# A decode layer on one core: the folded sum added in PSUM by an identity product, and the last columns split 192/64

## The chip, the core and the metric

The kernel runs on one core of a Trainium2 chip. The metric is the device time of one execution, in microseconds (us); of several runs the median is given. One core has five engines with instruction queues of their own: TensorE (PE in the profile; PEld is its weight load), VectorE (DVE), ScalarE (ACT), GpSimd (POOL) and SyncE (SP). They meet through semaphores. Data move between HBM and the on-chip memory SBUF by transfers (DMA) that SP and ACT issue here; products of TensorE are summed in PSUM, which has eight banks of 512 fp32 columns in 128 partitions.

## What is computed

One decode step of a transformer layer, all in fp32, for 8 sequences of one token and a model width of 1024:

```python
h  = x + attention(layernorm(x))      # 32 query heads, 4 key/value heads, window of 1024 keys
h2 = h + ffn(layernorm(h))            # h2 is the output, 8 x 1024

def ffn(x):                           # Dm = 1024, Df = 3584
    g = x @ w_gate
    u = x @ w_up
    return (gelu(g) * u) @ w_down     # the change lies at the end of this product
```

## The kernel before, in words

**Weights stream in, once.** The weights and the cache are laid out on the host in one array, in the order in which they are used. SP loads them through two halves of one SBUF tile `w` (`load`, L237): 14 large passes (`PASSES`, L28) that alternate between the halves, and behind them, without a wait, four small pieces for the rest of `w_down` (L259 to L261). A pass's load waits until the products of the pass two earlier are done (L239). The order on SP's queue is written out by hand, and so is that of every other engine.

**Products.** All matrix products have the small operand (8 rows, padded to 32) as weights and the streamed matrix as the moving operand. Four products sit side by side in the array, each with 32 output columns of its own, so that one "group" of four writes the four 32-partition quarters of a bank (`products`, L158). Such a product is called tiled here. fp32 takes two passes, and the trace shows each as a MATMUL of its own with a LDWEIGHTS before it. TensorE runs a loop of seven turns (L171 to L197), each with one pass of either half and eight transposes between them (L183). The transposes use the array whole (128 weights columns), so they are not tiled; only two of the seven turns use their results, which go to banks 4 and 5.

**The down product.** The 3584 rows of `w_down` are 28 chunks of 128 rows. Chunks 0 to 23 (`PAIRED = 24`) are the passes d0 and d1, in pairs of half the columns, so that their results must be folded: the upper 64 partitions of a bank hold, for the other half of the columns, what has to be added to the lower 64, and the other way round. The last four chunks, 24 to 27, come in the four small pieces, as "single row chunks": each of the four quarters of a bank gets 256 (`QW`) of the 1024 output columns, so nothing is folded. `PARTS = (2, 1)` says that the first piece has chunks 24 and 25, the second chunk 26. Chunk 27 is split by columns over the last two pieces: columns 0 to 159 of every quarter (`CUT = 160`) and columns 160 to 255. The semaphores of the four pieces are `s_dn[0]` to `s_dn[3]`.

**The end, before the change.**

- TensorE sums chunks 24 to 26 in bank 7 (L218 to L224, products at L221), then multiplies chunk 27 into bank 4 (160 columns) and bank 5 (96 columns), each after its own piece (L226 to L234, products at L229).
- `folded` (L384) puts the results of d0, d1 and the residual h together: two adds on DVE, a copy each on ACT (L389) and POOL (L390) that move halves across partitions, and an add on DVE into `pre` (L392, called at L459).
- DVE then adds bank 7 onto `pre` (L460), and adds `pre` and bank 4 into the first part of `o_fin` (L464), `pre` and bank 5 into the second (L466).
- ACT issues the output transfer of the first part (L480), SP that of the second (L483). ACT and POOL report to SP, which clears the semaphores and waits for both transfers (L485 to L488).

DVE's instructions are recorded and put down at the end, so all of them have the line L98 in the profile; they are told apart by tile and shape.

```python
226      for i, (b, c0, n) in enumerate(fin):      # fin = [(4, 0, CUT), (5, CUT, QW - CUT)]
...
230                  bank(b)[32 * j:32 * j + 32, 0:n], at_[:, rows - 1, :], w[:, at:at + n],
231                  start=True, stop=True), (s_dn[len(PARTS) + i], 16), inc=False)
```

Of the kernel before, what the change touches and what calls it, by code (L numbers as in the profile page):

```python
# [8 lines left out]
P = 128  # L9
# [7 lines left out]
NQ = 4  # L17
QW = D // NQ
# [1 line left out]
HB = B // 2  # L20
HALF = 16384
GAP = 144
CUT = 160

# [6 lines left out]
PAIRED = 24  # L33
PARTS = (2, 1)
# [81 lines left out]
def decode_block(nc, out, x, srcs, W):  # L116
# [3 lines left out]
    def sb(name, shape):  # L120
        return nc.alloc_sbuf_tensor(name, list(shape), F32).ap()

    first = nc.alloc_semaphore("first")
    pe = Engine(nc, nc.tensor, "pe")
    vector = Noted(nc.vector)
    dve = Engine(nc, vector, "dve")
    act = Engine(nc, nc.scalar, "act")
# [3 lines left out]

    s_in = [nc.alloc_semaphore(f"s_in{s}") for s in range(2)]
    s_dn = [nc.alloc_semaphore(f"s_dn{i}") for i in range(len(PARTS) + 2)]
    s_fin = nc.alloc_semaphore("s_fin")
    s_end = nc.alloc_semaphore("s_end")
    s_out = nc.alloc_semaphore("s_out")

    w = sb("w", [P, 2 * HALF])
    st = [sb(f"st{s}", [P, D + 32]) for s in range(2)]
    p_sb = sb("p", [P, W])  # L140
    ident = sb("ident", [P, P])
    at_ = sb("at", [P, DF // P, 32])
# [4 lines left out]
    def bank(i, n=1):  # L147
        return banks[:, i * N:(i + n) * N]
# [9 lines left out]
    def products(s, c):  # L158
        for j in range(NQ):
            at = block(s, c, j)  # L160
            ins = nc.tensor.matmul(  # L161
                bank(2 * s + c // 4)[32 * j:32 * j + 32, :],
                st[s][:, (c * NQ + j) * 32:(c * NQ + j + 1) * 32], w[:, at:at + N],
                start=(c % 4 == 0), stop=(c % 4 == 3))
        return ins
# [5 lines left out]
    with nc.body("turns", valid_engines=on_pe):  # L171
        closing = nc.tensor.mark_branch_hint_location()
        take(s_in[0], 17)
        for c in range(NC):
            if c == 4:
                take(s_half0, 16)
            ins = products(0, c)
        ins.then_inc(pe.sem, 1)
        take(s_p, 1)
        for h in range(2):  # L180
            for i in range(KC // 2):
                c = h * KC // 2 + i
                ins = nc.tensor.transpose(pp[h][:, i], p_sb[:, c * P:(c + 1) * P], ident)  # L183
            ins.then_inc(pe.sem, 1)
        take(s_in[1], 18)
        for c in range(4):
            if c == 3:
                take(s_half1, 16)
            ins = products(1, c)
# [3 lines left out]
    with nc.body("upper", valid_engines=on_pe):  # L193
        for c in range(4, NC):
            ins = products(1, c)
# [4 lines left out]
    def done(name):  # L200
        t, s = divmod(PASSES.index(name), 2)
        return (pe.sem, 5 * t + ((5 if t < TURNS - 1 else 4) if s else 1))
# [6 lines left out]
    rows = DF // P  # L209
    at = HALF + HALF // 2  # L210
    tail_at, place, of = [], [], []
    for i, n in enumerate(PARTS):
        tail_at.append(at)
        for k in range(n):
            place.append(at + k * D)
            of.append((s_dn[i], 16))
        at += n * D
    for q in range(PAIRED, rows - 1):  # L218
        for j in range(NQ):
            k = place[q - PAIRED] + j * QW  # L220
            ins = pe(lambda e: e.matmul(  # L221
                bank(7)[32 * j:32 * j + 32, 0:QW], at_[:, q, :], w[:, k:k + QW],
                start=(q == PAIRED), stop=(q == rows - 2)), of[q - PAIRED], inc=False)
    t_quads = pe.mark(ins)  # L224
    fin = [(4, 0, CUT), (5, CUT, QW - CUT)]
    for i, (b, c0, n) in enumerate(fin):  # L226
        tail_at.append(at)
        for j in range(NQ):
            ins = pe(lambda e: e.matmul(  # L229
                bank(b)[32 * j:32 * j + 32, 0:n], at_[:, rows - 1, :], w[:, at:at + n],  # L230
                start=True, stop=True), (s_dn[len(PARTS) + i], 16), inc=False)
            at += n
        t = pe.mark(ins)
        fin[i] += (t,)  # L234
# [29 lines left out]
    t = pool(lambda e: e.memset(ident, 0.0))  # L264
# [6 lines left out]
    t = pool(lambda e: e.memset(p_sb, 0.0))  # L271
# [48 lines left out]
    for hf in range(2):  # L320
        q_sb = sb(f"q{hf}", [P, N])
        t = dve(lambda e: e.tensor_scalar(q_sb, bank(2 * hf), scale, None, op0=ALU.mult), done(f"q{hf}"))
        t = dve(lambda e: e.scalar_tensor_tensor(
            q_sb, bank(2 * hf + 1), scale, q_sb, op0=ALU.mult, op1=ALU.add), t)
# [28 lines left out]
    for hb in range(2):  # L353
        nmax = sb(f"nmax{hb}", [P, 1])
        t = dve(lambda e: e.tensor_reduce(
            out=nmax, in_=bank(0, 2), axis=AX.X, op=ALU.max, negate=True), done(f"k{hb}"))
        tot = sb(f"tot{hb}", [P, 1])
        t = act(lambda e: e.activation(p_sb, bank(0, 2), AF.Exp, bias=nmax, accum_out=tot), t)  # L358
# [7 lines left out]
        else:  # L366
# [4 lines left out]
        t = dve(lambda e: e.tensor_add(o_sum, o_sum, bank(3)), act(lambda e: e.copy(o_sum, bank(2)), done(f"v{hb}")))  # L371
        o_sb = sb(f"o{hb}", [P, DH])
        t = dve(lambda e: e.tensor_scalar(
            o_sb, o_sum[:, 0:DH], share[hb][:, 0:1], None, op0=ALU.mult), t)
        for b in range(1, HB):
            t = dve(lambda e: e.scalar_tensor_tensor(
                o_sb, o_sum[:, b * DH:(b + 1) * DH], share[hb][:, b:b + 1], o_sb,
                op0=ALU.mult, op1=ALU.add), t)
# [5 lines left out]
    def folded(name, total, deps, into, others):  # L384

        ex = sb(name + "_ex", [P, QW])
        far, near = total[:, QW:N], total[:, 0:QW]
        t = dve(lambda e: e.tensor_add(far, far, others[:, QW:N]), *deps)
        t0 = act(lambda e: e.copy(ex[0:64], far[64:P]), t)  # L389
        t1 = pool(lambda e: e.tensor_copy(ex[64:P], far[0:64]), t)  # L390
        t = dve(lambda e: e.tensor_add(near, near, others[:, 0:QW]), *deps)
        return dve(lambda e: e.tensor_add(into, near, ex), t, t0, t1)  # L392
# [3 lines left out]
    t = act(lambda e: e.copy(y_sum, bank(0)), done("o0"))  # L396
    t = pool(lambda e: e.tensor_add(y_sum[:, 0:QW], y_sum[:, 0:QW], x_sb), t)  # L397
    t = dve(lambda e: e.tensor_add(y_sum, y_sum, bank(1)), t)
    t = dve(lambda e: e.tensor_add(y_sum, y_sum, bank(2)), t, done("o1"))
# [38 lines left out]
    t = dve(lambda e: e.tensor_mul(h1[:96], ge[1][:96], h1[:96]), t_g1, t_u1)  # L438

    n = UPPER * 32  # L440
# [7 lines left out]
    t = dve(lambda e: e.tensor_mul(h0, ge[0], h0), t_g0, t_u0)  # L448
# [5 lines left out]
    d_sum = sb("d_sum", [P, N])  # L454
    t = act(lambda e: e.copy(d_sum, bank(0)), done("d0"))
    t = pool(lambda e: e.tensor_add(d_sum[:, 0:QW], d_sum[:, 0:QW], h_sb), t)  # L456
    t = dve(lambda e: e.tensor_add(d_sum, d_sum, bank(1)), t)
    pre = sb("pre", [P, QW])
    t = folded("d", d_sum, (t, done("d1")), pre, bank(2))  # L459
    t_pre = dve(lambda e: e.tensor_add(pre, pre, bank(7)[:, 0:QW]), t, t_quads)  # L460
    o_fin = sb("o_fin", [P, QW])
    parts = [o_fin[:, c0:c0 + n] for b, c0, n, t in fin]
    b, c0, n, t = fin[0]
    t0 = dve(lambda e: e.tensor_add(parts[0], pre[:, c0:c0 + n], bank(b)[:, 0:n]), t, t_pre)  # L464
    b, c0, n, t = fin[1]
    dve(lambda e: e.tensor_add(parts[1], pre[:, c0:c0 + n], bank(b)[:, 0:n]), t, inc=False).then_inc(s_fin, 1)  # L466

    on_dve = [nc.vector.engine]
    turn = nc.alloc_registers("turn_v", engines=on_dve)
# [9 lines left out]
    act.wait(t0)  # L479
    nc.scalar.dma_start(out[:, 0:CUT], parts[0]).then_inc(s_out, 16)  # L480
    nc.scalar.wait_ge(s_fin, 1).then_inc(s_end, 1)
    nc.sync.wait_ge(s_fin, 1)
    nc.sync.dma_start(out[:, CUT:QW], parts[1]).then_inc(s_out, 16)  # L483

    nc.gpsimd.wait_ge(*t_pre).then_inc(s_end, 1)  # L485
    nc.sync.wait_ge(s_end, 2).then_inc(s_end, -2)
    nc.sync.sem_clear(range(first.num, s_fin.num + 1))
    nc.sync.wait_ge(s_out, 32).then_inc(s_out, -32)  # L488
# [95 lines left out]
```

## Time and profile before

| | before |
|---|---|
| median of three runs | 264.04 us (263.79 to 264.05) |
| the profiled execution, its own time | 263.77 us |
| its span in the profile | 262.5 us |
| granted TensorE clock, mean of the core | 0.771 |
| TensorE busy (products) | 136.8 us, 52% of the span |
| DVE / ACT / POOL busy | 35.9 / 19.1 / 6.8 us |
| read from HBM | 111.18 MB, 424 GB/s over the span |

The span runs from the first to the last event that the profile has of the core; the execution's own time is 1.27 us more. The rest of this document counts time from the span's start. In the profile "out<-in" names the tile written and the tiles read, "128*32 128x256" is a product with 128x32 weights and a moving operand of 128x256, and "<-" in brackets names what ended an idle time of the engine. The end of a matmul is modelled, its start is recorded.

### The profile page before, as it was taken

How to read it: one execution, taken by the hardware profiler on the slowest of the kernel's cores; microseconds unless marked ns; L12 is line 12 of the kernel's file. 1: busy time of each engine (PE TensorE's matmuls, PEld its weight loads, DVE VectorE, ACT ScalarE, POOL GpSimd, SP SyncE). 2: the span in 40 equal slices, each digit the busy share in tenths (PEclk: the TensorE clock that was granted, in tenths of full speed). 3: DMA queues.
4: the chain of work that ended last, by engine and by line, in shares of the span. 5: the costliest groups of instructions: out<-in, count | busy, mean ns of one | idle time of the engine just before them, and what ended most of it. 6: DMA issues, size and time to landing. Idle time of an engine off the chain costs nothing. (4 is left out here: it accounts for less than half of the span.)

```text
span 262.5 us, 2187 instructions
## 1 busy us (share of the span) xinstructions
PE 136.8 (52%) x960; PEld 42.6 (16%) x960; DVE 35.9 (14%) x98; ACT 19.1 (7%) x28; POOL 6.8 (3%) x16
## 2 busy tenths in 40 slices
PE   0005905806826607627708608539277590585954
PEld 0001301201222102122102202112121130121321
DVE  0060110120130210110120100450101004003013
ACT  1030000000020000110000000210401010000000
POOL 2000100000000000000000100000000001001010
PEclk9999975955865965955956965957959598586899
DMA  8998997999899799989979989997999999799996
GB/s 320 484 410 390 479 479 340 459 479 410 390 479 479 340 459 479 420 380 479 479 330 469 479 380 420 479 479 320 479 434 405 439 479 479 320 454 424 439 390 230
DMA packets 3216, 111.31 MB, mean 424 GB/s; under 512 B 496, under 2 KB 784, under 8 KB 1040
## 3 DMA queue, kind: packets, MB, share of 16 engines
q1 hardware_dynamic: 3024, 111.20, 98.4%
q10 hardware_dynamic: 192, 0.11, 0.1%
HBM read 111.18 MB, written 0.13 MB: 424 GB/s over the span
## 5 line engine op out<-in xcount | busy, mean ns | idle before, releaser
L161 PE MATMUL banks<-w,st 128*32 128x512 f32 x864 | 125.3, 743 | 115.7 <-PEq L156 115.7
L161 PEld LDWEIGHTS banks<-w,st 128*32 128x32 f32 x864 | 34.3, 133 | 201.4 <-issue 201.4
L183 PE MATMUL banks<-ident,p 128*128 128x128 f32 x56 | 9.3, 321 | 6.3 <-PEq L156 6.3
L183 PEld LDWEIGHTS banks<-ident,p 128*128 128x128 f32 x56 | 7.4, 164 | 12.3 <-issue 12.3
L358 ACT ACTIVATE p<-banks,nmax 128x1024 f32<-128x1024 f32 x2 | 2.2, 1113 | 73.5 <-DVE nmax L98 73.5
L98 DVE TENSOR_REDUCE nmax<-banks 128x1 f32<-128x1024 f32 x2 | 2.5, 1225 | 33.8 <-PE banks L161 33.8
L98 DVE TENSOR_TENSOR y_sum<-y_sum,banks 128x512 f32<-128x512 f32 (+1 forms) x4 | 2.1, 552 | 33.6 <-PE banks L161 17.8
L98 DVE TENSOR_SCALAR q<-banks 128x512 f32<-128x512 f32 x2 | 1.4, 692 | 31.3 <-PE banks L161 31.3
L98 DVE TENSOR_TENSOR o_sum<-o_sum,banks 128x512 f32<-128x512 f32 x2 | 1.4, 690 | 29.5 <-ACT o_sum L371 29.5
L98 DVE TENSOR_TENSOR d_sum<-d_sum,banks 128x256 f32<-128x256 f32 (+1 forms) x3 | 1.4, 509 | 17.3 <-POOL d_sum L456 12.1
L397 POOL TENSOR_TENSOR y_sum<-y_sum,x_sb 128x256 f32<-128x256 f32 x1 | 0.7, 722 | 115.7 <-ACT y_sum L396 115.7
L422 POOL COPY st<-at 128x768 f32<-128x768 f32 (+2 forms) x3 | 1.8, 609 | 68.4 <-DVE at L98 68.4
L371 ACT COPY o_sum<-banks 128x512 f32<-128x512 f32 x2 | 1.2, 586 | 26.8 <-PE banks L161 26.8
L98 DVE TENSOR_TENSOR u0s<-u0s,banks 128x512 f32<-128x512 f32 x1 | 0.7, 689 | 16.3 <-ACT u0s L412 16.3
L98 DVE TENSOR_TENSOR g0s<-g0s,banks 128x512 f32<-128x512 f32 x1 | 0.7, 689 | 15.8 <-ACT g0s L412 15.8
L292 ACT ACT_TABLE_LOAD x2 | 2.6, 1283 | 1.7 <-POOL ident L264 1.6
L98 DVE TENSOR_TENSOR u1s<-u1s,banks 96x512 f32<-96x512 f32 x1 | 0.7, 683 | 14.0 <-ACT u1s L415 14.0
L221 PE MATMUL banks<-w,at 128*32 128x256 f32 x24 | 1.7, 387 | 1.5 <-DMA w<-weights 1.5
L313 ACT COPY st<-ln_t 128x1024 f32<-128x1024 f32 x2 | 2.1, 1046 | 5.1 <-DVE ln_t L98 5.1
L98 DVE TENSOR_TENSOR g1s<-g1s,banks 96x512 f32<-96x512 f32 x1 | 0.7, 682 | 10.9 <-ACT g1s L415 10.9
L98 DVE SCALAR_TENSOR_TENSOR o<-o_sum,share,o 128x128 f32<-128x128 f32 x6 | 2.1, 352 | 0.2
L412 ACT COPY u0s<-banks 128x512 f32<-128x512 f32 x1 | 0.6, 585 | 18.7 <-PE banks L161 18.7
(64 smaller groups left out, 39.5 us busy)
## 6 DMA issues: line engine op xcount, KB each, us to landing
w<-weights SPq DMA_DIRECT2D x2, 6144.0 KB, 23.5
w<-weights SPq DMA_DIRECT2D x2, 4096.0 KB, 24.5
w<-weights SPq DMA_DIRECT2D x1, 3072.0 KB, 17.0
w<-weights SPq DMA_DIRECT2D x2, 1024.0 KB, 20.1
w<-weights SPq DMA_DIRECT2D x1, 512.0 KB, 21.9
w<-weights SPq DMA_DIRECT2D x1, 320.0 KB, 22.3
w<-weights SPq DMA_DIRECT2D x1, 192.0 KB, 22.3
w<-weights SPq DMA_DIRECT2D x10, 28.9
```

The source lines that it names most:

```text
L98: ins = getattr(self.eng, n.name)(*n.args, **n.kw)
L161: ins = nc.tensor.matmul(bank(2 * s + c // 4)[32 * j:32 * j + 32, :], st[s][:, (c * NQ + j) * 32:(c * NQ + j + 1) * 32], w[:, at:at + N], ...
L183: ins = nc.tensor.transpose(pp[h][:, i], p_sb[:, c * P:(c + 1) * P], ident)
L221: ins = pe(lambda e: e.matmul(bank(7)[32 * j:32 * j + 32, 0:QW], at_[:, q, :], w[:, k:k + QW], start=(q == PAIRED), stop=(q == rows - 2)), ...
L292: t = act(lambda e: e.activation(sd, ve, AF.Sqrt), t_ve)
L313: act(lambda e: e.copy(to[1], wide), t, inc=False).then_inc(s_in[1], 2)
L358: t = act(lambda e: e.activation(p_sb, bank(0, 2), AF.Exp, bias=nmax, accum_out=tot), t)
L371: t = dve(lambda e: e.tensor_add(o_sum, o_sum, bank(3)), act(lambda e: e.copy(o_sum, bank(2)), done(f"v{hb}")))
L397: t = pool(lambda e: e.tensor_add(y_sum[:, 0:QW], y_sum[:, 0:QW], x_sb), t)
L412: t = act(lambda e: e.copy(out[:nb], bank(b)[:nb]), done(name))
L422: return nc.gpsimd.tensor_copy(st[s][:, at:at + n * 64].rearrange("p (c x m) -> p c x m", c=n, x=2), at_[:, c0:c0 + n].unsqueeze(2).to_bro ...
```

## The change

Bank 7 and the add of it go. Chunks 24 to 26 are now multiplied straight into banks 4 and 5, in two groups of 192 and 64 columns each; chunk 27 is added there too, with `start=False`. `pre`, the folded sum, is added in the same banks by two products with the identity matrix (128 weights columns, not tiled), placed on TensorE's queue between chunk 25 and chunk 26. TensorE waits for `pre` by a new semaphore `s_pre`, which POOL raises when DVE has written `pre`. What is left at the end is a copy out of PSUM: the first 192 columns by ACT, the last 64 by DVE. The pieces of chunk 27 and the two output transfers are cut at 192 in place of 160. POOL's report to SP waits for the products of the first part in place of `pre`.

```diff
-CUT = 160
+CUT = 192
...
+    s_pre = nc.alloc_semaphore("s_pre")
...
+    fin = [(4, 0, CUT), (5, CUT, QW - CUT)]
+    pre = sb("pre", [P, QW])
     for q in range(PAIRED, rows - 1):
-        for j in range(NQ):
-            k = place[q - PAIRED] + j * QW
-            ins = pe(lambda e: e.matmul(
-                bank(7)[32 * j:32 * j + 32, 0:QW], at_[:, q, :], w[:, k:k + QW],
-                start=(q == PAIRED), stop=(q == rows - 2)), of[q - PAIRED], inc=False)
-    t_quads = pe.mark(ins)
-    fin = [(4, 0, CUT), (5, CUT, QW - CUT)]
+        if q == rows - 2:
+            for b, c0, n in fin:
+                pe(lambda e: e.matmul(
+                    bank(b)[:, 0:n], ident, pre[:, c0:c0 + n], start=False, stop=False), (s_pre, 1), inc=False)
+        for b, c0, n in fin:
+            for j in range(NQ):
+                k = place[q - PAIRED] + j * QW + c0
+                pe(lambda e: e.matmul(
+                    bank(b)[32 * j:32 * j + 32, 0:n], at_[:, q, :], w[:, k:k + n],
+                    start=(q == PAIRED), stop=False), of[q - PAIRED], inc=False)
...
                 bank(b)[32 * j:32 * j + 32, 0:n], at_[:, rows - 1, :], w[:, at:at + n],
-                start=True, stop=True), (s_dn[len(PARTS) + i], 16), inc=False)
+                start=False, stop=True), (s_dn[len(PARTS) + i], 16), inc=False)
...
-    pre = sb("pre", [P, QW])
-    t = folded("d", d_sum, (t, done("d1")), pre, bank(2))
-    t_pre = dve(lambda e: e.tensor_add(pre, pre, bank(7)[:, 0:QW]), t, t_quads)
+    t_pre = folded("d", d_sum, (t, done("d1")), pre, bank(2))
+    nc.gpsimd.wait_ge(*t_pre).then_inc(s_pre, 1)
...
-    t0 = dve(lambda e: e.tensor_add(parts[0], pre[:, c0:c0 + n], bank(b)[:, 0:n]), t, t_pre)
+    t0 = act(lambda e: e.copy(parts[0], bank(b)[:, 0:n]), t)
...
-    dve(lambda e: e.tensor_add(parts[1], pre[:, c0:c0 + n], bank(b)[:, 0:n]), t, inc=False).then_inc(s_fin, 1)
+    dve(lambda e: e.tensor_copy(parts[1], bank(b)[:, 0:n]), t, inc=False).then_inc(s_fin, 1)
...
-    nc.gpsimd.wait_ge(*t_pre).then_inc(s_end, 1)
+    nc.gpsimd.wait_ge(*fin[0][3]).then_inc(s_end, 1)
```

## Rows read from the trace of the kernel before

**Rows 1.** The page, part 3: queue, packets, bytes, share of 16 engines' span.

```profile
q1 hardware_dynamic: 3024, 111.20, 98.4%
```

**Rows 2.** The chain that ended last: start in us, length in us, what.

```profile
237.35 22.27 DMA w<-weights
...
259.66 0.52 PE banks L229 x8
...
260.28 0.54 DVE o_fin L98 x2
```

**Rows 3.** The timeline from 244 to 262.5: start, length, engine, line, operation.

```profile
249.06 0.59 ACT L455 COPY d_sum<-banks 128x512 f32<-128x512 f32 x1 [12.92 <-PE banks L161]
249.73 0.72 POOL L456 TENSOR_TENSOR d_sum<-d_sum,h_sb 128x256 f32<-128x256 f32 x1 [10.38 <-ACT d_sum L455]
...
257.35 0.43 DVE L98 TENSOR_TENSOR pre<-d_sum,d_ex 128x256 f32<-128x256 f32 x1 [0.24 <-POOL d_ex L390]
...
257.56 1.07 PE L221 MATMUL banks<-w,at 128*32 128x256 f32 x16 [1.25 <-DMA w<-weights]
...
258.83 0.64 PE L221 MATMUL banks<-w,at 128*32 128x256 f32 x8 [0.20 <-DMA w<-weights]
259.54 0.42 DVE L98 TENSOR_TENSOR pre<-pre,banks 128x256 f32<-128x256 f32 x1 [1.76 <-PE banks L221]
...
260.12 0.16 PEld L229 LDWEIGHTS banks<-w,at 128*32 128x32 f32 x8 [0.30 <-DMA w<-weights]
...
260.63 0.35 ACTq L480 DMA_DIRECT2D out<-o_fin  x1
260.85 0.35 SPq L483 DMA_DIRECT2D out<-o_fin  x1
```

**Rows 4.** The DMA issues: count, KB each, median us from issue to landing.

```profile
w<-weights SPq DMA_DIRECT2D x1, 320.0 KB, 22.3
w<-weights SPq DMA_DIRECT2D x1, 192.0 KB, 22.3
...
out<-o_fin ACTq DMA_DIRECT2D x1, 80.0 KB, 1.6
out<-o_fin SPq DMA_DIRECT2D x1, 48.0 KB, 1.6
```

**Rows 5.** Short stretches of PE's timeline at the end; x4 is one tiled group.

```profile
257.80 0.61 PE L221 MATMUL banks<-w,at 128*32 128x256 f32 x8
...
258.23 0.40 PE L221 MATMUL banks<-w,at 128*32 128x256 f32 x4
...
259.82 0.32 PE L229 MATMUL banks<-w,at 128*32 128x160 f32 x4
...
260.23 0.27 PE L229 MATMUL banks<-w,at 128*32 128x96 f32 x4
```

**Rows 6.** The same view where tiled products give way to transposes, 247.9 to 249.3.

```profile
247.94 0.64 PE L161 MATMUL banks<-w,st 128*32 128x512 f32 x4
...
248.37 0.64 PE L161 MATMUL banks<-w,st 128*32 128x512 f32 x4
...
248.94 0.33 PE L183 MATMUL banks<-ident,p 128*128 128x128 f32 x1
...
249.10 0.49 PE L183 MATMUL banks<-ident,p 128*128 128x128 f32 x3
...
249.21 0.38 PE L183 MATMUL banks<-ident,p 128*128 128x128 f32 x2
```

**Rows 7.** Groups by line and shape, ACT and DVE: busy us, mean ns of one.

```profile
L313 ACT COPY st<-ln_t 128x1024 f32<-128x1024 f32 x2 | 2.1, 1046 | 5.1 <-DVE ln_t L98 5.1
...
L389 ACT COPY d_ex<-d_sum 64x256 f32<-64x256 f32 x1 | 0.4, 403 | 7.2 <-DVE d_sum L98 7.2
...
L98 DVE TENSOR_TENSOR o_fin<-pre,banks 128x160 f32<-128x160 f32 x1 | 0.3, 322 | 0.3 <-PE banks L229 0.3
...
L98 DVE TENSOR_TENSOR o_fin<-pre,banks 128x96 f32<-128x96 f32 x1 | 0.3, 256 | 0.0
```

## The prediction, made before the changed kernel had run

> **What bounds the kernel now.** I read the page's DMA part first. One queue, SP's, is busy for 98.4% of the span on average over the 16 engines [rows 1]. The kernel is a stream of weights with computation beside it, so nothing before the last piece can be moved by this change: it touches no load ahead of chunk 27, and the four pieces keep their sum of bytes. What can move is the tail, from the last landings to the end.
>
> The chain that ended last tells the tail's order [rows 2]: the piece with the first 160 columns lands at 237.35 + 22.27 = 259.62, its products start at 259.66, DVE's two adds run from 260.28 to 260.82. The timeline [rows 3] fills in the rest. The weights for the last 96 columns are loaded at 260.12, again after a DMA: so the last piece landed at about 260.08. ACT issues its output transfer at 260.63, SP at 260.85; each lands 1.6 us after its issue [rows 4], so SP's, the later, ends the span at 260.85 + 1.6 = 262.45 of 262.5. From the last landing of data to the end there are only 262.45 − 260.08 = 2.37 us, and 1.6 of them are the output's flight. That caps what any rearrangement here can win.
>
> **The change, part by part.**
>
> The length of tiled groups first. A group of 512 columns starts 248.37 − 247.94 = 0.43 us after the one before it [rows 6], one of 256 columns (258.23 − 257.80)/2 = 0.215 us [rows 5]; both are 0.84 ns a column. The two 160-column groups start 259.82 − 259.66 = 0.16 us apart, the two 96-column ones 260.23 − 260.12 = 0.11 [rows 2, 3, 5], a little over proportion. So a group of 192 columns takes between 0.161 (by proportion) and 0.178 (on the line from 160 to 256); I take 0.17. A group of 64 takes between 0.054 (by proportion) and 0.11 (that of 96); I take the middle, 0.08.
>
> *Chunks 24 to 26 in two banks.* Each was two groups of 256, 0.43 us; it becomes two of 192 and two of 64: 2 × (0.17 + 0.08) = 0.50. The first piece still lands just before 257.56 [rows 3]. Chunks 24 and 25 then stream until 257.56 + 0.02 (the first distance, 257.80 − 257.56, is that much longer) + 1.00 = 258.58.
>
> *The new wait for `pre`.* DVE ends the fold at 257.35 + 0.43 = 257.78 [rows 3]. POOL's relay is one semaphore hop to POOL and one to TensorE; the nearest row is POOL starting at 249.73 on what ACT ended at 249.06 + 0.59 = 249.65, 0.08 us [rows 3]. Two such hops give 257.94, at least 0.6 us before TensorE comes to the identity products. Behind the wait on TensorE's queue stand chunks 26 and 27, that is everything that sets the end, but the cover is 0.6 us of products of chunks 24 and 25. I cost the wait at nothing. On POOL nothing but the final report is queued behind it.
>
> *The identity products.* Two products of two passes: 192 columns twice, 2 × 0.17; 64 columns twice, at the distance of untiled products of 128 columns, 249.21 − 249.10 = 0.11 [rows 6], since each has 128 weights columns to load: 0.22. Sum 0.56 (0.43 by proportion at the least).
>
> *Two changes between tiled and whole use of the array.* The trace has one way of it back to back [rows 6]: the last tiled group starts at 248.37 and streams 0.43, until 248.80; the first transpose starts at 248.94, and the next one 0.16 later where the rest keep 0.11. So the way in costs 0.14 + 0.05 = 0.19. The way back the trace doesn't show, since the loop always waits for data there; I take 0.19 for it too, by the row it is nearest to. The bounds for each way are nothing, and a whole modelled product of 0.64 [rows 6]. [...]
>
> *TensorE's sum.* 258.58 + 0.19 + 0.56 + 0.19 = 259.52. Chunk 26 has landed by then (it ran at 258.83 before [rows 3]); it takes 0.50, until 260.02. Chunk 27's first piece grows from 320 to 384 KB: 192 KB came in 260.08 − 259.62 = 0.46 us, so 64 KB more take 0.15 and it lands at 259.77, the last one at 260.08 as before. TensorE would be ready for it 0.21 us too late, at 260.02 in place of 259.81. Its two 192-column groups stream until 260.36, the two of 64 until 260.52. The slack that the kernel before had on TensorE here (it idled 0.20 and 0.19 us before the pieces) is used up.
>
> *The copies.* A reader of PSUM starts 0.26 us after the end of the streaming: ACT at 249.06 after 248.80, DVE at 259.54 after 258.83 + 0.02 + 0.43 = 259.28 [rows 3, 6]; I take 0.27. ACT copies 512 columns in 0.59 [rows 3], and its copies of 1024 and 256 columns differ by (1046 − 403)/768 = 0.84 ns a column [rows 7]: 192 columns take 0.59 − 320 × 0.84 ns = 0.32. DVE's adds of 160 and 96 columns differ by 1.03 ns a column [rows 7], so 64 columns take 0.22; the copy reads the same bank, I price it as the add. ACT: 260.36 + 0.27 + 0.32 = 260.95, its issue 0.03 later (the gap from DVE's first add, 260.28 + 0.32, to 260.63 [rows 2, 3, 7]) at 260.98. DVE: 260.52 + 0.27 + 0.22 = 261.01, SP's issue at 261.04. The output's rows become 96 and 32 KB; 80 and 48 KB took the same 1.6 us [rows 4], so the size is worth nothing.
>
> *What goes at no gain.* DVE's add of bank 7 (0.42 us at 259.54 [rows 3]) lay beside the wait for chunk 27 and its products, until 260.28; two adds of 0.32 and 0.26 in a row become two copies on two engines, but DVE's second add stood only some 0.04 behind its data.
>
> *The sum.* The end moves from 260.85 + 1.6 to 261.04 + 1.6: +0.19 us. The profiled execution took 263.77, so 263.96; it lies 0.27 under the median of the runs, 264.04, to which I add the same: **264.23 us**. A measurement of this kernel can tell about 0.2% (0.53 us) from no change, so I forecast no change.
>
> The bounds. *Least:* no cost of switching, everything by proportion: TensorE is through with chunk 26 by 259.3 and waits for the piece at 259.81; 0.34 and 0.11 later the streams end at 260.15 and 260.26; SP issues at 260.78, −0.07, 263.97 us. *Most:* 0.64 for each switch, 0.178 and 0.11 a group: chunks 24 and 25 end at 258.73, the identity products at 259.95, chunk 26 at 261.16, chunk 27 at 261.74; with 0.33, 0.26 and 0.03 behind it SP issues at 262.36, +1.51, 265.55 us.
>
> **The rivals.**
>
> *It fits into TensorE's slack.* Without a cost of the way back (the array may take tiled weights at once) TensorE is late by 0.02 only, and the end stands where it stood: 264.0 us, −0.07 to +0.03. For it: the least bound, and that weights are loaded ahead everywhere else. Against it: the 0.14 of idle array in rows 6.
>
> [...] If the two switches take over 0.72 us together, where I have 0.38, the end is later by over 0.53 us, more than 0.2%; at the 0.64 each of the upper bound it is 265.55 us. [...] For it: the way back was never seen. Against it: the way in cost a third of that. It would need a stall of TensorE of half a microsecond that no row has.
>
> *Faster.* The stream would have to end earlier. The smallest tail, from 260.08 on, is 0.04 + 0.11 + 0.27 + 0.22 + 0.03 + 1.6 = 2.27 us against 2.37 now, so the products and copies can't win more than 0.1 us; a gain of over 0.53 us, to under 263.5, needs a change in the landings, from last rows of 1 KB in place of 1.5 KB a partition. Nothing in the rows speaks for it.
>
> *The change does not do what it says:* if `pre` were late after all, TensorE would stand before chunk 26. From 258.77 on each 0.1 us costs 0.1; that needs a relay over 0.9 us where hops take 0.08. I count it with the slower case.
>
> **How the numbers follow.** The forecast's case (0 to +0.5 us) gets 0.60, the slack rival 0.25, the slower ones 0.11, the faster one 0.04. The first two are both within 0.2%: 0.85. The three runs lie 0.26 us apart, so the range goes from the slack rival less 0.22, 263.75, to the point where the drain would begin to show, 264.75.
>
> **What would show it right or wrong.** In the changed profile the two identity products should start near 258.8, in two groups of rows with 128x192 and 128x64; chunk 26's first product about 0.75 us later; the first product of chunk 27 should not wait for its DMA, but follow chunk 26 at 260.0; ACT's issue should come within 0.1 us of SP's, both near 261.0; the output still takes 1.6 us. A wait of TensorE for POOL, a gap of over 0.5 us at the identity products, or a last landing more than 0.1 us from 260.08 would make the working wrong.

## The result, and the profile after

| | before | after |
|---|---|---|
| median (range) of 22 runs each | 263.99 us (263.79 to 264.14) | 264.18 us (264.02 to 264.99) |
| ratio of the times, 95% interval | | 1.0014 (1.0008 to 1.0020) |
| profiled execution, its span | 263.77, 262.5 us | 264.18, 262.9 us |

By the medians the change costs 0.19 us (a ratio of 1.0007); the ratio in the table weighs all runs, the few high ones named below too. The cost is clear of the noise, but under the 0.2% that was set as the bound for "no change". The forecast was +0.19 us and no change. The number came true; the step that was to bring it did not, as the profile shows.

The timeline of the changed kernel from the folded sum to the last issue, to be held against [rows 3]:

```profile
257.58 0.42 DVE L98 TENSOR_TENSOR pre<-d_sum,d_ex 128x256 f32<-128x256 f32 x1 [0.24 <-POOL d_ex L398]
...
257.78 1.08 PE L231 MATMUL banks<-w,at 128*32 128x192 f32 x32 [1.25 <-DMA w<-weights]
...
258.79 0.76 PE L226 MATMUL banks<-pre,ident 128*128 128x192 f32 x4
...
259.48 0.64 PE L231 MATMUL banks<-w,at 128*32 128x192 f32 x16
...
260.02 0.64 PE L237 MATMUL banks<-w,at 128*32 128x192 f32 x16
...
260.62 0.32 ACT L471 COPY o_fin<-banks 128x192 f32<-128x192 f32 x1 [3.17 <-PE banks L237]
260.73 0.22 DVE L98 COPY o_fin<-banks 128x64 f32<-128x64 f32 x1 [2.73 <-PE banks L237]
260.97 0.37 ACTq L487 DMA_DIRECT2D out<-o_fin  x1
260.99 0.35 SPq L490 DMA_DIRECT2D out<-o_fin  x1
```

Everything here is 0.2 us later than in the rows of before, chunk 24's first product too (257.78 against 257.56 [rows 3]), where nothing has been changed yet. The first DVE instruction, which waits for x, shows where that comes from. The first of the two fences is the timeline of before, the second that of after:

```profile
12.92 0.43 DVE L98 BATCH_NORM_STATS2 ln_bn<-x_sb 128x6 f32<-128x256 f32 x1 [10.88 <-DMA x_sb<-x]
```

```profile
13.15 0.43 DVE L98 BATCH_NORM_STATS2 ln_bn<-x_sb 128x6 f32<-128x256 f32 x1 [11.11 <-DMA x_sb<-x]
```

The shift of 0.23 is there at 13 us. The profiled execution of before lay 0.22 under the median of its runs, that of after on it: this is how executions differ, not the change. So the two tails are compared from chunk 24's first product on. (The page rounds the span to 0.1 us, half of the cost that is looked for. The trace has it to the nanosecond, 262.455 and 262.865 us, and that is used from here on.)

| from chunk 24's first product | before | after | difference |
|---|---|---|---|
| chunk 27's first product | 2.10 | 2.24 | +0.14 |
| ACT's issue | 3.07 | 3.19 | +0.12 |
| SP's issue | 3.29 | 3.21 | −0.08 |
| end of the span | 4.90 | 5.09 | +0.19 |

The last issue comes sooner and the end later. What grew is the flight of the output, as the DMA issues of after show (KB each, median us from issue to landing), where the kernel before had 1.6 and 1.6 [rows 4]:

```profile
out<-o_fin ACTq DMA_DIRECT2D x1, 96.0 KB, 1.7
out<-o_fin SPq DMA_DIRECT2D x1, 32.0 KB, 1.8
```

Before, ACT's issue stood 0.22 us ahead of SP's [rows 3]; after, 0.02. Theory A, formed here, says that the two transfers hold each other up, so that the end is counted from the first issue. (Both raise one semaphore, and the page's two landings are the times when 16 and all 32 of its reports are in, 262.63 and 262.83 in after; with both under way they do not tell which transfer landed first.) Theory B is the prediction's: TensorE is late, and each transfer flies 1.6 us.

One thing more is in the runs. Five of the 22 lie at 264.67 to 264.99, the other 17 at 264.02 to 264.42 with a median of 264.15; no run of before is over 264.14 here. Beside the experiments below, four of 78 runs of before lie over 264.3, the highest at 264.55. (The expectations below say six; it is five.)

### The profile page after: what moved, and what is told of

The parts are those of the page before. It is cut to its first block, busy times and chain, and to the rows that moved or that the text cites. A ratio compares the mean times of both kernels' runs of the same rounds, so it can differ in the third digit from the quotient of the medians.

```text
span 262.9 us, 2241 instructions
## 1 busy us (share of the span) xinstructions
PE 134.5 (51%) x988; PEld 43.0 (16%) x988; DVE 35.2 (13%) x96; ACT 19.4 (7%) x29; POOL 6.8 (3%) x16
## 5 line engine op out<-in xcount | busy, mean ns | idle before, releaser
L162 PE MATMUL banks<-w,st 128*32 128x512 f32 x864 | 123.5, 734 | 118.5 <-PEq L157 118.5
L184 PE MATMUL banks<-ident,p 128*128 128x128 f32 x56 | 8.5, 300 | 6.3 <-PEq L157 6.3
L184 PEld LDWEIGHTS banks<-ident,p 128*128 128x128 f32 x56 | 6.7, 152 | 12.3 <-issue 12.3
L231 PE MATMUL banks<-w,at 128*32 128x192 f32 (+1 forms) x48 | 1.7, 276 | 1.2 <-DMA w<-weights 1.2
```

Of the source, the lines that this page charges most:

```text
L162: ins = nc.tensor.matmul(bank(2 * s + c // 4)[32 * j:32 * j + 32, :], st[s][:, (c * NQ + j) * 32:(c * NQ + j + 1) * 32], w[:, at:at + N], ...
L231: pe(lambda e: e.matmul(bank(b)[32 * j:32 * j + 32, 0:n], at_[:, q, :], w[:, k:k + n], start=(q == PAIRED), stop=False), of[q - PAIRED], i ...
```

## The experiments

All medians stand beside runs of the kernel before on the same chip, at 263.91 to 263.96. The changed kernel was not run again beside them; its 264.18 and 1.0014 are from the table above.

**Take the identity products out** (of the changed kernel).

```diff
-        if q == rows - 2:
-            for b, c0, n in fin:
-                pe(lambda e: e.matmul(
-                    bank(b)[:, 0:n], ident, pre[:, c0:c0 + n], start=False, stop=False), (s_pre, 1), inc=False)
```

> The changed kernel without the two identity products and without TensorE's wait for the folded sum (so the output lacks that sum). Theory A, shared output: the end is set by the two output transfers, whose packets go through the same 16 DMA engines for some 0.55 us from the first one's start on; TensorE waits for the piece with chunk 27 anyway, so taking 0.7 us of work off it changes nothing: the same time as the changed kernel within 0.1 us, about 0.2 us over the kernel before, and chunk 27's first product still starts about 2.24 us after chunk 24's. Theory B, the prediction's: the identity products and the switches make TensorE late by 0.2 us: without them the time falls by about 0.2 us, back to that of the kernel before.

Measured: 264.13 us, ratio 1.0009 (1.0001 to 1.0018). Its timeline:

```profile
257.61 1.08 PE L227 MATMUL banks<-w,at 128*32 128x192 f32 x32 [1.25 <-DMA w<-weights]
...
258.89 0.64 PE L227 MATMUL banks<-w,at 128*32 128x192 f32 x16 [0.20 <-DMA w<-weights]
...
259.88 0.64 PE L233 MATMUL banks<-w,at 128*32 128x192 f32 x16 [0.35 <-DMA w<-weights]
```

Without them TensorE waits for its pieces, and chunk 27 starts 259.88 − 257.61 = 2.27 us after chunk 24, as with them (2.24). The identity products lie in waiting time. In the time the case is less clear, since the interval of the ratio begins close to the 1.0000 that B asked for; the profile decides it, and B falls.

**Hold the first transfer back in the kernel before.**

```diff
-    nc.scalar.dma_start(out[:, 0:CUT], parts[0]).then_inc(s_out, 16)
     nc.scalar.wait_ge(s_fin, 1).then_inc(s_end, 1)
+    nc.scalar.dma_start(out[:, 0:CUT], parts[0]).then_inc(s_out, 16)
```

> The kernel before, with ACT's output transfer held back until the last part is written, so that both transfers are issued together, some 0.22 us later for ACT's and at the same moment as ever for SP's. Theory A, shared output: the data of both take the 0.55 us from then on, so the end moves by about +0.2 us (ratio about 1.0008). Theory B, a flight of 1.6 us of each transfer by itself: the end is SP's issue plus 1.6 us, nothing moves (0 to +0.05 us).

Measured: 264.17 us, +0.23, ratio 1.0012 (1.0003 to 1.0021). In its timeline SP issues as ever (3.29 us after 257.69), ACT 0.10 behind it:

```profile
260.98 0.35 SPq L483 DMA_DIRECT2D out<-o_fin  x1
261.08 0.35 ACTq L481 DMA_DIRECT2D out<-o_fin  x1
```

Nothing else differs from the kernel before: losing the head start of 0.22 us of one transfer costs 0.23 us, as theory A has it, where B expected nothing.

**Cut the changed kernel at 160.**

```diff
-CUT = 192
+CUT = 160
```

> The changed kernel cut at 160 columns in place of 192. Theory A, shared output: the first part is written some 0.15 us earlier (160 columns land, stream and copy sooner), the last part 0.1 us later; the first transfer leaves earlier and the end comes about 0.1 us before that of the changed kernel. Theory B, fixed flight: the last issue is 0.1 us later, and so is the end: +0.1 us on the changed kernel.

Measured: 263.95 us, ratio 1.0005 (0.9996 to 1.0014). Nine runs have a median of 263.94, the kernel before's, and none of them is over 263.98, where the 17 low runs of the change begin at 264.02. The median is 0.23 under that of the change, twice what A expected and against B. Three of 12 runs are at 264.75 to 264.87. The profiled execution, at 264.87, is one of these, and it shows what they are. Stretches of it (engine columns, then the granted clock, the DMA share and GB/s last):

```profile
253.00:254.00 1.00, 0.98 (x8) 0.37 (x12) 0.00 (x0) 0.00 (x0) 0.00 (x0) 0.50 1.00 418
...
255.00:256.00 1.00, 1.00 (x8) 0.22 (x4) 0.00 (x0) 0.00 (x0) 0.00 (x0) 0.50 1.00 418
```

and of its timeline:

```profile
253.02 5.16 PE L162 MATMUL banks<-w,st 128*32 128x512 f32 x32 [2.63 <-PEq L157]
...
259.23 0.43 DVE L98 TENSOR_TENSOR pre<-d_sum,d_ex 128x256 f32<-128x256 f32 x1 [0.23 <-POOL d_ex L398]
...
259.76 0.73 PE L226 MATMUL banks<-pre,ident 128*128 128x160 f32 x4 [0.71 <-POOLq L467]
```

After 2.63 us without work the granted clock stands at 0.50, and the last products of d1 take 5.16 us where the profiled run of after, at 1.00 there, needs 3.64. So the folded sum is written at 259.66 in place of 258.0, and TensorE stands 0.71 us at the identity products with chunks 26 and 27 behind it. The idle time alone does not decide the clock: after has 2.65 us without work in the same place and keeps 1.00. The stream of weights, the obvious rival, is not late in this run: by the trace its last piece lands 237.48 us after its first, against 237.50 in the kernel before.

**Write a quarter of the output** (changed kernel).

```diff
-    nc.scalar.dma_start(out[:, 0:CUT], parts[0]).then_inc(s_out, 16)
+    nc.scalar.dma_start(out[0::4, 0:CUT], parts[0][0::4]).then_inc(s_out, 16)
...
-    nc.sync.dma_start(out[:, CUT:QW], parts[1]).then_inc(s_out, 16)
+    nc.sync.dma_start(out[0::4, CUT:QW], parts[1][0::4]).then_inc(s_out, 16)
```

> The changed kernel, writing only the 32 partitions of the output that hold a sequence's result (every fourth), in place of all 128: a quarter of the output's packets and bytes, the rest of the output array is left as it is. Theory A, shared output: the output's data take about 0.15 us in place of 0.55, the end comes 0.3 to 0.4 us sooner: about 263.8 us, faster than the kernel before by 0.15 us. Theory B, fixed flight of 1.6 us: no change, about 264.2 us.

Measured: 264.26 us, ratio 1.0015 (1.0006 to 1.0024), two of 11 runs at 264.64 and 265.30: a miss for A's arithmetic. Its issues are longer (0.37 and 0.35 after):

```profile
260.80 0.52 ACTq L487 DMA_DIRECT2D out<-o_fin  x1
260.81 0.54 SPq L490 DMA_DIRECT2D out<-o_fin  x1
```

The DMA packets in the trace show what A left out. The data do take less: 0.22 us for ACT's part and 0.17 for SP's, one behind the other, where in after the two together take 0.58. But they start later. ACT's first packet starts 1.18 us after its issue and SP's 1.43, where in after the first of either starts 0.85 to 0.92 us after its issue. The later start eats the gain, and the end comes 2.02 us behind the first issue, against 1.90.

**Make the folded sum late,** in the changed kernel and in the kernel before (the same edit in `folded`).

```diff
+        if name == "d":
+            more = sb("more", [P, QW])
+            for i in range(4):
+                t = dve(lambda e: e.tensor_add(more, near, near), t)
         return dve(lambda e: e.tensor_add(into, near, ex), t, t0, t1)
```

> The changed kernel with four more adds of 128x256 on DVE (into a tile that nothing reads) ahead of the last add of the fold, so that the folded sum comes about 1.8 us later. Theory W, the wait decides once the sum is late: TensorE stands before chunk 26 with everything behind it. The sum reaches TensorE some 0.8 us before it is needed and 0.1 us more lies before chunk 27's piece, so about 1.8 - 0.9 = 0.9 us come through: about 265.1 us, with a gap of some 1 us at the identity products. Theory N, the wait has cover to spare (up to the last landing, 2 us later): no change, 264.2 us.

> The kernel before with the same four adds in the same place. There the folded sum is needed by DVE's add of bank 7 only, at 259.54, 1.76 us after it is written, and nothing on TensorE waits for it. Theory W: the delay of 1.8 us is covered, the time stays within 0.1 us of the kernel before (263.95 us); so the same lateness that costs the changed kernel 0.9 us costs this one nothing. A rival by which the delay costs through the adds themselves would show +0.9 us here too.

Measured: 265.05 us in the changed kernel, ratio 1.0042 (1.0029 to 1.0056); 263.92 in the kernel before, ratio 1.0005 (0.9993 to 1.0017). Theory W holds in both medians: +0.87 on 264.18, and nothing. One of the 11 runs of the second is at 265.53; it would fit a run in which the sum is late by the slow clock and by the adds together, more than the 1.76 us to spare, but it was not profiled. The profiled execution of the first is its slowest, 266.43 us: TensorE waits for the sum, and its granted clock falls to 0.50 behind the wait, as its timeline and stretches show.

```profile
259.82 1.33 PE L226 MATMUL banks<-pre,ident 128*128 128x192 f32 x4 [0.94 <-POOLq L471]
```

```profile
260.00:261.00 1.00, 1.00 (x4) 0.96 (x4) 0.00 (x0) 0.00 (x0) 0.00 (x0) 0.50 0.00 0
```

**One output transfer** (changed kernel; SP waits for ACT's copy too).

```diff
-    nc.scalar.dma_start(out[:, 0:CUT], parts[0]).then_inc(s_out, 16)
...
-    nc.sync.dma_start(out[:, CUT:QW], parts[1]).then_inc(s_out, 16)
+    nc.sync.dma_start(out, o_fin).then_inc(s_out, 16)
```

> The changed kernel with one output transfer of all 256 columns, issued by SP when both copies are done, in place of two that are issued within 0.02 us. Theory A, shared output: the data of 128 rows of 1 KB take some 0.35 us in place of 0.55 for 256 shorter rows, so the end comes about 0.2 us sooner, near 263.95 us. Theory C, the write's round trip is fixed and the number of transfers plays no part: no change, 264.2 us.

Measured: 264.34 us, ratio 1.0019 (1.0008 to 1.0030), but five of 11 runs lie at 264.72 to 265.08; the other six have a median of 264.05. In the profile the span ends 1.74 us after the only issue, where after ended 1.88 us after the last; the data take 0.52 us, not the 0.35 that A expected. The one issue comes later, 3.30 us after chunk 24's first product against 3.19 for the first of two. It gives back some 0.1 us at most: between A (0.2) and C (nothing), and not settled by this run.

**The identity products behind the loop over chunks 24 to 26, cut at 160.**

```diff
-CUT = 192
+CUT = 160
...
-        if q == rows - 2:
-            for b, c0, n in fin:
-                pe(lambda e: e.matmul(
-                    bank(b)[:, 0:n], ident, pre[:, c0:c0 + n], start=False, stop=False), (s_pre, 1), inc=False)
...
+    for b, c0, n in fin:
+        pe(lambda e: e.matmul(
+            bank(b)[:, 0:n], ident, pre[:, c0:c0 + n], start=False, stop=False), (s_pre, 1), inc=False)
```

> The changed kernel cut at 160 columns, with the identity products behind chunk 26 in place of ahead of it. By theory A the cut at 160 alone gave back the 0.2 us (263.95 us); by theory W the later place leaves chunk 26 out of what a late sum holds up. So the typical run stays at 263.95 us, equal to the kernel before within 0.1 us, and the runs far above the median (some 0.8 us in the changed kernel and with the cut at 160) come down to 0.5 us or less above it. Against W: such runs stay at 264.8 us.

Measured: 264.30 us (264.05 to 264.45), ratio 1.0011 (1.0002 to 1.0020). No run is high, as W has it (with five in 22 as the rate, 11 runs without one happen by chance in some 6% of cases, an estimate), but the typical one is 0.35 worse than with the cut alone, which I had not expected:

```profile
259.68 0.73 PE L231 MATMUL banks<-pre,ident 128*128 128x160 f32 x4
...
260.35 0.65 PE L236 MATMUL banks<-w,at 128*32 128x160 f32 x16
```

Ahead of chunk 26 the identity products fill the wait for its piece; behind it they push chunk 27 to 260.35 − 257.84 = 2.51 us after chunk 24, against 2.10 in the kernel before, which has the same cut. Here TensorE does set the end. The identity products start 1.84 us after chunk 24, later than the late sum let them in the profile of the cut at 160 (259.76 − 257.99 = 1.77), so such a sum would cost nothing here.

**Keep TensorE busy in its gap** (ten, then five products a turn; changed kernel, and cut at 160).

```diff
+        for i in range(10):
+            nc.tensor.matmul(bank(7)[:, 0:P], ident, ident, start=True, stop=True)
         take(s_in[1], 18)
```

> The changed kernel with ten more products of the identity with itself (into bank 7, which nothing reads) in every turn of TensorE's loop, between the transposes and the wait for the second half's pass; there TensorE idles 2.65 us in the last turn. They add 2.2 us of TensorE work a turn in waiting time. Theory W with the clock: the runs at 264.7 to 265.0 us (6 of 22) are those in which the granted clock is 0.50 while the last products of d1 run, so that the folded sum is 1.6 us late and TensorE waits for it; kept busy, TensorE keeps its clock there, so the typical run stays at 264.15 us and no run lies above 264.5. Rival: those runs are late for a reason outside TensorE (the stream of weights); then a quarter of the runs still lies 0.7 us above the rest.

> The same ten products, cut at 160 columns in place of 192. Theory W with the clock: typical run at 263.95 us as with the cut at 160 alone, which had 3 of 12 runs at 264.75 to 264.87, and none of those: a change that costs nothing against the kernel before (ratio 1.000 within 0.0005). Rival: a quarter of the runs still near 264.8 us.

> The changed kernel with five of the ten products of the identity with itself in every turn, so 1.1 us of TensorE work in waiting time and 20 TensorE instructions fewer than with ten. With ten, TensorE's last products stood 2.6 to 2.8 us with no wait shown, while one packet of instructions was loaded (267.16 us). Theory P, the length of the program: the stall comes from the place of the last instructions in TensorE's program, 12 of which stood behind it; with 20 fewer it is gone and no packet of instructions shows: 264.15 us. Rival: the stall comes from the added work itself; half of it then leaves about half, some 265.6 us. On the clock (theory W): no run above 264.5 us in place of 6 of 22.

> The same five products with the cut at 160 columns. Theory P: no stall, the typical run at 263.95 us, as with the cut at 160 alone; the rival: about 265.6 us. On the clock: no run near 264.8 us, where the cut at 160 alone had 3 of 12.

Measured: 267.16 and 267.28 us with ten, 266.19 and 265.89 with five; all four miss the time. In the first, the ten products are more than fill: d1's last products start at 254.11 (252.89 in after), and TensorE waits 0.48 us for the sum. Then it stands still amid chunk 27's products, with no wait shown, and the list of queues has a new one:

```profile
260.49 0.60 PE L239 MATMUL banks<-w,at 128*32 128x192 f32 x10
...
263.70 0.44 PE L239 MATMUL banks<-w,at 128*32 128x64 f32 x6 [2.61 <-issue]
```

```profile
q8 instruction: 1, 0.02, 0.0%
```

One packet of instructions, 0.02 MB, is loaded from 261.04 to 262.30 us; neither the kernel before nor the changed one has such a packet in its span. With five products (cut at 192) the stall leaves the products (ACT issues at 260.79, SP at 260.80), but the packet stays, from 261.74 to 263.31. Of the 32 reports of the output, 30 are in by 262.65, and the last two come at 264.41 and 264.57; 9 of the 144 packets of either transfer run after 263: as if the packet held up one of the 16 engines with its share of either transfer, which is an inference. Part of the added time even lies outside the span: time and span differ by 1.5 to 1.7 us in four of the five runs and by 3.19 in the fifth, against 1.3 to 1.4 in the kernel before.

So theory P fails as it stood: 20 instructions fewer moved the stall and did not take it away. Its rival, that half the work leaves about half, asked for 265.6 us and is missed too, by 0.6 and 0.3. The length of the program and the added work were not separated. On the clock, the 18 runs of the four kernels spread by 0.8 us at most within each and show no group 0.7 above the rest; since the packet is in the profile of each, and their medians lie 1.9 us or more above those of the kernels they were made from, that settles nothing.

## Why the prediction was right, and where it was not

The sum came out at +0.19 and 0.19 was measured, from other terms. SP's issue came 0.08 us sooner, where 0.19 later was forecast, and the way from it to the end took 0.27 longer, where nothing was forecast. That the two numbers agree is luck.

*TensorE's sum* is the step that failed. It was to reach chunk 27 0.21 us too late. Measured from chunk 24's first product, the identity products start at 258.79 − 257.78 = 1.01 (predicted 1.21), chunk 26 at 1.70 (1.96), chunk 27 at 2.24 (2.46). In short stretches of PE's timeline of after:

```profile
258.62 0.24 PE L231 MATMUL banks<-w,at 128*32 128x64 f32 x4
258.79 0.43 PE L226 MATMUL banks<-pre,ident 128*128 128x192 f32 x1
...
259.06 0.38 PE L226 MATMUL banks<-pre,ident 128*128 128x192 f32 x2
...
259.22 0.33 PE L226 MATMUL banks<-pre,ident 128*128 128x64 f32 x2
...
259.27 0.28 PE L226 MATMUL banks<-pre,ident 128*128 128x64 f32 x1
...
259.48 0.36 PE L231 MATMUL banks<-w,at 128*32 128x192 f32 x3
```

What was mis-sized is everything with 64 columns. The two tiled groups of 64 ahead of the identity products start at 258.56 and 258.62, so one takes 0.055 us, in proportion, where 0.08 was taken; four of them in chunks 24 and 25 make 0.10. The two identity passes of 64 start at 259.22 and 259.27, 0.055 us apart, where 0.11 was taken for each "since each has 128 weights columns to load"; that makes 0.11. Together these are 0.21 of the 0.26 us by which chunk 26 came sooner, as much as TensorE was to be late.

The changes between tiled and whole use of the array were priced about right, 0.19 each. On the way in the array is idle for 0.11 us (the last tiled group streams until 258.68), and the first identity pass takes 0.27 where the second takes 0.16: 0.22 in all, counted as the prediction counted it. On the way back, which the trace of before could not show, 0.15 us pass from the end of the last identity pass, at about 259.33, to chunk 26. So the trace shows the array idle at both changes, for 0.11 and 0.15 us, but not what fills that time. The drain that the upper end of the prediction's range names is shown by no run; in its place the runs show these two times and the 0.14 us before the first transpose in the kernel before [rows 6].

The slack rival, given 0.25, names the outcome for TensorE: it needed nothing that it did not have. Chunk 27's piece lands at 259.98 by the trace, and its first product starts 0.04 us later, as in the kernel before and in the one without identity products. Its reason, a way back without a cost, is not what was seen. Taking the products out moved nothing.

*The copies* were right: 0.32 for ACT (0.32 measured), 0.22 for DVE (0.22). With TensorE in time, SP's issue came 0.08 sooner, at the rival's bound of −0.07.

*The flight of the output* is the term that was mis-sized. "80 and 48 KB took the same 1.6 us, so the size is worth nothing" read two landings that were staggered by 0.22 us as if each stood alone. The kernels with two transfers of all 128 partitions that no instruction packet disturbs, from their issues and unrounded spans in the trace (us; stagger is the distance between the issues):

| | cut | stagger | last issue to end | first issue to end |
|---|---|---|---|---|
| before | 160 | 0.21 | 1.61 | 1.82 |
| before, late sum | 160 | 0.22 | 1.60 | 1.82 |
| changed, cut at 160 | 160 | 0.13 | 1.69 | 1.82 |
| changed, identity products behind chunk 26 | 160 | 0.13 | 1.69 | 1.82 |
| before, first held back (SP issues first) | 160 | 0.10 | 1.76 | 1.86 |
| changed, late sum | 192 | 0.12 | 1.79 | 1.90 |
| changed, no identity products | 192 | 0.02 | 1.88 | 1.90 |
| after | 192 | 0.02 | 1.88 | 1.90 |

The end lies 1.82 to 1.90 us behind the first issue, and a second transfer up to 0.22 us later rides along free. What the two share is the DMA engines, which are full while the output moves. The first two stretches are of before, the third is of after (the last three numbers are granted clock, DMA share and GB/s):

```profile
261.60:261.70 0.10, 0.00 (x0) 0.00 (x0) 0.00 (x0) 0.00 (x0) 0.00 (x0) 1.00 1.14 365
...
261.80:261.90 0.10, 0.00 (x0) 0.00 (x0) 0.00 (x0) 0.00 (x0) 0.00 (x0) 0.50 1.00 220
```

```profile
262.10:262.20 0.10, 0.00 (x0) 0.00 (x0) 0.00 (x0) 0.00 (x0) 0.00 (x0) 1.00 0.97 284
```

At 261.60 to 261.70 ACT's transfer is alone, since SP's first packet starts at 261.72. In before the first packet starts 0.85 us after the first issue, the data of both take 0.56, and the span ends 0.41 behind the last packet; in after these are 0.86, 0.58 and 0.45. With the engines full, the earlier start of the second transfer (issued 0.02 us behind the first in after, 0.22 in before) did not shorten the data.

So the +0.19 us has two parts. The first issue comes 0.12 later: 192 columns land, stream and copy later than 160, and the last 64 gain nothing by being early. And the way from the first issue to the end is 0.07 longer (1.895 against 1.821). That part goes with the cut, staggered or not, as the table shows (the row in which SP issues first lies between); what causes it is not shown. That the head start is worth 0.2 us is shown by holding ACT's transfer back in the kernel before (+0.23), and that the cut is the cost by the cut at 160 in the changed one (back to 263.95).

*The wait for the sum.* "I cost the wait at nothing" holds in most runs, and the cover too: at least 0.6 us were forecast, the rows of after have 258.79 − 258.00 less a relay of 0.10 (259.72 to 259.82 in the late sum), and 1.8 us of delay let 0.87 through. What the prediction left out is that the lateness of the sum varies from run to run with the granted clock: in the one high run that was profiled, d1's last products are 1.5 us longer. The kernel before has room for that, since its folded sum had 1.76 us to spare [rows 3] (late sum there: 263.92). The changed one puts it on TensorE's queue ahead of two chunks. The chain is shown in one profile, that of the cut at 160, and by the two late sums; that all five high runs of the change are of this kind was not seen. Their mean granted clocks hint at it: 0.786 or 0.806, values that none of the other 17 runs has, though a mean does not say when the clock was low. Against it, one run of 11 without the wait, that without the identity products, also lay at 264.74.

*No version is faster than the kernel before.* The best is the cut at 160, equal to it in its typical run and worse in a quarter of its runs.

## What to carry to other kernels

Where two output transfers end a kernel, look at when the first is issued before balancing the parts: here the end followed the first issue by 1.82 to 1.90 us, a second transfer up to 0.22 us later ended with it, and two equal finishes (192 and 64 columns, 264.18 us) cost more than an uneven pair (160 and 96, 263.95 us). Read differences of 0.1 us from unrounded times, not from a span given to 0.1. A term of the sum that comes from two events in one trace ("both took 1.6 us") holds for their arrangement, and has to be asked again where the change alters that. And a sum that a side engine adds late can absorb a variation of an earlier stage (in the kernel before it had 1.76 us to spare): moved onto TensorE's queue, ahead of the last chunks, it lets that variation, 1.6 us in the run that was profiled, through to the end as far as it exceeds the cover.

## What the runs showed of the hardware that was not expected

Instructions added to TensorE's loop cost time here even where their work lay in waiting time. Five products a turn, ten MATMULs with their weight loads in the program, took 1.28 us of TensorE in six of the seven turns (2.34 in the third) and left 1.53 us of waiting behind them in the last turn (1.30 cut at 160); they came with one packet of 0.02 MB of instructions in the tail and some 2 us of time (266.19 against 264.18 us, cut at 160 265.89 against 263.95). Ten products came with a stop of TensorE of 2.61 us, with six MATMULs still to go. What brings the packet in, no run shows: the length of the program and the work grew together.

Picking every fourth partition made an output transfer slower to issue (0.52 and 0.54 us against 0.37 and 0.35) and later to start its data (1.18 and 1.43 us after the issue against 0.85 to 0.92), so that a quarter of the bytes ended no sooner.
